# Weights split by columns beside A and B, v by key blocks loaded first, attention spread as 12 places over the first A and 20 over the first B

## The chip, the cores and the metric

The kernel runs on one core of a Trainium2 chip. A core has TensorE (PE: matmuls, with its weight loads listed apart as PEld), VectorE (DVE), ScalarE (ACT), GpSimd (POOL) and SyncE (SP), each with its own queue of instructions, which it works off in order, and 16 DMA engines. SyncE here only issues DMAs. The metric is the device time of one execution in microseconds (us), the median of several runs. The profile is of one such execution.

## What is computed

Three stages, each feeding the next. Attention for 4 batches of 8 heads, 576 positions, head size 64, in two parts that are added: a dense one over positions averaged by fours (144 of them), and a local one in which each query sees the keys less than 4 positions away. Then a gated feed-forward block whose gate is a convolution over 3 positions, then a second one with a causal convolution over 5 positions.

```python
q_d = q.reshape(B, H, Sd, 4, D).mean(axis=3)          # k_d, v_d alike
out_d = sm_attn(q_d, k_d, v_d)                        # 144 x 144 softmax attention
mask = np.abs(pos[:, None] - pos[None, :]) < 4
attn = softmax(where(mask, scale * q @ k.T, -1e9))
x = np.repeat(out_d, 4, axis=2) + attn @ v            # (4, 576, 512) after the heads are joined
h = np.maximum(x @ w_in, 0.0)                         # A: 512 -> 1024
conv_out = sum(conv_w[k] * hp[:, k:k + S] for k in range(3))
y = (h * sigmoid(conv_out)) @ w_out                   # B: 1024 -> 512
gate_pre = sum(conv_w2[k] * yp[:, k:k + S] for k in range(5))
out = (sigmoid(gate_pre) * (y @ w_val)) @ w_out2      # C and D: 512 -> 512 each
```

The weight matrices are 64-bit floats in memory; q, k and v are 32-bit.

## The kernel before

**Precision.** Every large product is made of three: a matrix is split into a high part (rounded to the fast 32-bit matmul type) and a low part (the rest), and high x high, high x low and low x high are summed (`mm3`). A 64-bit weight piece is first turned into a 32-bit float by integer operations (`to_f32`: one ACT and four DVE operations on 128 x 512) and then split by one ACT copy (high) and one DVE subtraction (low). Such a piece with its six operations is called a split below.

**Weights.** The class `Weights` holds a list of jobs, 16 in all: 8 pieces of 128 rows x 512 columns of w_in (tiles win0 and win1 for high and low), then 8 of w_out (wout0, wout1). `load` issues the DMA of the next piece (512 KB) into a staging tile called stage, on SyncE's queue; `split` does the six operations on the oldest staged piece. The staging tiles take turns in the three buffers y1, y2, y3 for the first nine pieces and in y3 and y2 behind that, so a load must wait until the split of the piece that had its buffer is over.

**Attention.** It runs in 16 steps s, one for each pair of heads (4 for each batch), of 8 slots i each (`att_slots`): slot 0 the local scores (sl, 96 small matmuls in a masked PSUM tile), slot 1 the dense scores (sd), slots 2 and 3 the local product with v of the step before (avl, in two halves; it needs the value windows ldw: 32 keys for each block of 24 queries) and the softmax normalisations, slots 4 and 5 the transposes of the next step's k and q (tp) and its pooled values (ldv, vd), slots 6 and 7 the transposes of the probabilities (et, etd) and the dense product (avd). The results are xo, split into xhi and xlo.

**A and B.** For each batch 32 units: A has 16 (8 column blocks f of w_in, two units each; behind the second, ACT and DVE make relu, convolution, gate and the split into hghi and hglo, DVE's part being cv three times and hglo), B has 16 (4 column blocks e of w_out, four units each; the fourth needs hghi and hglo of f = 6 and 7). A matmul of A is called pa, one of B pb. `step_unit` issues one unit, and ahead of it one `split` and one `load` where its rule says so.

**Order.** The main loop at the end runs the steps and slots. With s = 4, i = 5 the first unit is issued, and from there on one unit after each slot: 32 slots for the 32 units of batch 0 beside the attention of batch 1, then 32 slots for those of batch 1, and so on. Ahead of that, the attention of batch 0 runs without units, and `EARLY` names the slots behind which a split and a load are issued. `ordered` makes the instructions that a function issues stand behind the last ones of the named engines. `split` in `step_unit` is called outside of `ordered`, so the tile framework's scheduler places its operations on their engines by its own estimate of when they can run.

**Loads at the start.** Before, SyncE issues k and q of all four head pairs with v in two halves among them, the conv weights, three weight pieces, then `load_vw_first`: 24 loads of 64 KB, the value windows of batch 0 (6 groups g x 4 partition blocks c), then the first loads of batch 1. A DMA queue has 8 semaphores in turn, so a load waits for the eighth before it.

Behind all this (not touched): the units of batches 1 to 3 beside the attention of batches 2 and 3, then C and D.

## Time and profile before

| | us |
|---|---|
| median of 3 runs | 521.6 (517.53 to 523.5) |
| the profiled execution | 523.8 |
| its span, first to last instruction | 521.7 |
| PE busy | 453.0 (87%) |
| PEld busy | 412.7 (79%) |
| DVE busy | 358.2 (69%) |
| ACT busy | 266.0 (51%) |
| POOL busy | 6.1 (1%) |
| the 16 DMA engines, 39.58 MB | 76 GB/s over the span |

Times of rows are counted from the span's start. A row of a timeline gives start, duration, engine, line, operation, output<-inputs, shapes and count; a bracket at its end says how long the engine had stood idle before it and what it waited for. An engine that is busy most of the time need not be what limits a stage; what limits it is read from the chain of waits and from the rows around a wait.

### The profile page before, as it was taken

How to read it: one execution, taken by the hardware profiler on the slowest of the kernel's cores; microseconds unless marked ns; L12 is line 12 of the kernel's file. 1: busy time of each engine (PE TensorE's matmuls, PEld its weight loads, DVE VectorE, ACT ScalarE, POOL GpSimd, SP SyncE). 2: the span in 40 equal slices, each digit the busy share in tenths (PEclk: the TensorE clock that was granted, in tenths of full speed). 3: DMA queues.
4: the chain of work that ended last, by engine and by line, in shares of the span. 5: the costliest groups of instructions: out<-in, count | busy, mean ns of one | idle time of the engine just before them, and what ended most of it. 6: DMA issues, size and time to landing. Idle time of an engine off the chain costs nothing.

```text
span 521.7 us, 13808 instructions
## 1 busy us (share of the span) xinstructions
PE 453.0 (87%) x5961; PEld 412.7 (79%) x5961; DVE 358.2 (69%) x655; ACT 266.0 (51%) x564; POOL 6.1 (1%) x25
## 2 busy tenths in 40 slices
PE   5747565468977999899899999999968999999997
PEld 4546544357976999899899889999958999889885
DVE  3517678789997344897866799503989999964130
ACT  1504535467784443877545678414877365542122
POOL 4000000000000000000000000000000000000000
PEclk9955556598998999999799999999987999999999
DMA  8957124343441214224133121003112000120102
GB/s 204 222 130 164 52 82 114 113 132 111 119 113 29 67 43 93 48 58 98 28 74 79 37 64 32 14 21 122 40 41 81 10 33 2 60 102 20 62 21 102
DMA packets 70963, 39.58 MB, mean 76 GB/s; under 512 B 59050, under 2 KB 65526, under 8 KB 70902
## 3 DMA queue, kind: packets, MB, share of 16 engines
q1 hardware_dynamic: 70902, 38.70, 28.0%
q8 instruction: 47, 0.77, 0.6%
q14 instruction: 14, 0.11, 0.1%
HBM read 33.96 MB, written 4.72 MB: 74 GB/s over the span
## 4 chain that ended last, share of the span: by engine, by line
PE 59%; DVE 21%; DMA 9%; ACT 7%; SPq 2%; issue 1%; ACTq 0%; DVEq 0%
PE pb L141 19%; PE pa L141 12%; PE pc L141 10%; PE pd L141 10%; DVE cv L151 5%; DVE stage L151 4%; PE avl L141 3%; DMA ldv<-in_v_dram 3%; DMA stage<-in_moe_w_in_dram 2%; ACT ed L151 2%; DMA ldq<-in_q_dram 2%; DVE hglo L151 2%; SPq L283 1%; PE tp L141 1%; DMA stage<-in_moe_w_out_dram 1%
## 5 line engine op out<-in xcount | busy, mean ns | idle before, releaser
L141 PE MATMUL pb<-hghi,wout 128*128 128x288 f32 x512 | 105.5, 314 | 4.7 <-ACT hghi L151 4.7
L141 PE MATMUL pa<-xhi,win 128*128 128x288 f32 x512 | 103.0, 308 | 3.6 <-DVE xo L151 3.6
L141 PEld LDWEIGHTS pb<-hghi,wout 128*128 128x128 f32 x512 | 80.6, 197 | 8.6 <-ACT hghi L151 5.6
L141 PEld LDWEIGHTS pa<-xhi,win 128*128 128x128 f32 x512 | 78.1, 192 | 6.9 <-DVE xo L151 3.9
L141 PE MATMUL pb<-hglo,wout 128*128 128x288 f32 x256 | 57.5, 307 | 2.0 <-DVE hglo L151 2.0
L151 DVE SCALAR_TENSOR_TENSOR cv<-h,cwt,cv 128x576 f32<-128x576 f32 x64 | 51.9, 811 | 7.5 <-ACT cv L151 7.1
L141 PE MATMUL pa<-xlo,win 128*128 128x288 f32 x256 | 55.5, 299 | 0.0
L141 PE MATMUL pc<-ys,wval 128*128 128x288 f32 x384 | 51.3, 294 | 0.0
L141 PEld LDWEIGHTS pc<-ys,wval 128*128 128x128 f32 x384 | 51.1, 188 | 0.3
L151 DVE SCALAR_TENSOR_TENSOR g<-y,cwt,g 128x576 f32<-128x576 f32 x64 | 49.5, 814 | 0.0
L141 PEld LDWEIGHTS avl<-et,ldw 32*64 32x64 f32 x1536 | 30.1, 150 | 22.3 <-issue 8.5
L141 PE MATMUL avl<-et,ldw 32*64 32x24 f32 x1536 | 34.2, 227 | 15.5 <-DMA ldw<-in_v_dram 9.2
L141 PEld LDWEIGHTS pb<-hglo,wout 128*128 128x128 f32 x256 | 43.0, 197 | 3.5 <-DVE hglo L151 3.4
L141 PE MATMUL pd<-wout,hghi 128*128 128x512 f32 x144 | 44.7, 394 | 0.0
L141 PEld LDWEIGHTS pa<-xlo,win 128*128 128x128 f32 x256 | 42.0, 193 | 0.0
L151 DVE TENSOR_TENSOR xo<-avl,od 128x288 f32<-128x288 f32 x32 | 14.2, 444 | 32.3 <-PE avl L141 32.3
L151 ACT ACTIVATE ed<-ed,smd 72x144 f32<-72x144 f32 x64 | 21.4, 404 | 23.6 <-DVE smd L151 23.6
L141 PEld LDWEIGHTS pd<-wout,hghi 128*128 128x128 f32 x144 | 26.7, 187 | 6.3
L151 ACT ACTIVATE cv<-cv 128x576 f32<-128x576 f32 x32 | 21.9, 683 | 15.3 <-DVE cv L151 14.9
L151 DVE TENSOR_TENSOR hglo<-cv,hghi 128x576 fp32r<-128x576 f32 x32 | 24.1, 753 | 6.8 <-ACT hghi L151 6.8
L151 ACT ACTIVATE hghi<-cv 128x576 fp32r<-128x576 f32 x32 | 21.8, 680 | 13.0 <-DVE cv L151 12.9
L151 ACT ACTIVATE ed<-sd,mxd 72x144 f32<-72x144 f32 x64 | 23.3, 370 | 10.0 <-DVE mxd L151 9.2
(87 smaller groups left out, 695.2 us busy)
## 6 DMA issues: line engine op xcount, KB each, us to landing
stage<-in_moe_w_out_dram SPq DMA_DIRECT2D x12, 512.0 KB
out_dram<-o SPq DMA_DIRECT2D x18, 256.0 KB
stage<-in_moe_w_in_dram SPq DMA_DIRECT2D x8, 512.0 KB
ldv<-in_v_dram SPq DMA_DIRECT2D x13, 288.0 KB
ldk<-in_k_dram SPq DMA_DIRECT2D x26, 144.0 KB
ldq<-in_q_dram SPq DMA_DIRECT2D x26, 144.0 KB
ldw<-in_v_dram SPq DMA_DIRECT2D x48, 48.0 KB
stage<-in_moe_w_val_dram SPq DMA_DIRECT2D x4, 512.0 KB
```

The lines of the kernel that those rows point to most:

```text
L141: last["pe"] = nc.tensor.matmul(*a, **kw)
L151: last[self.key] = getattr(self.engine, name)(*a, **kw)
L283: nc.sync.dma_start(out=vw[KB * c : KB * c + KB, g], in_=v[0, :, k0 : k0 + KB].rearrange("h k d -> k h d"))
```

## The change

Five edits. The 16 weight pieces are cut by columns: a piece of w_in is now all 512 rows x 128 columns (one f), a piece of w_out 512 of its 1024 rows x 128 columns (half of one e); the bytes of a piece and the operations of a split stay the same, and a load now has 512 runs of 1 KB instead of 128 of 4 KB. The loads of pieces behind the first three are issued by POOL instead of SyncE. At the start, the value windows are loaded behind k and q of the first two head pairs and the first half of v; then come the three weight pieces, then k, q and v of the rest. `EARLY` has 4 entries instead of 8, and the 12 other splits are called at the units in `SPLITS`. The 16 units of batch 0's A are spread over 12 slots and the 16 of its B over 20, instead of 16 and 16; from unit 33 on the slots are the same as before.

```diff
-        def load(self):
+        def load(self, queue=nc.gpsimd):
             if not self.jobs:
                 return
-            dst, src, j, f0 = self.jobs.pop(0)
-            rows = src[j * 128 : j * 128 + 128]
+            dst, src, r0, nr, c0 = self.jobs.pop(0)
+            wide = PW // nr
+            rows = src[r0 * 128 : (r0 + nr) * 128]
...
-                nc.sync.dma_start(out=t, in_=rows.bitcast(I32)[:, 2 * f0 : 2 * (f0 + PW)])
-            self.staged.append((t, w, src.dtype == F32, dst, j, f0))
+                queue.dma_start(
+                    out=t.rearrange("p (r n) -> p r n", r=nr),
+                    in_=rows.bitcast(I32).rearrange("(r p) n -> p r n", p=128)[
+                        :, :, 2 * c0 : 2 * (c0 + wide)
+                    ],
+                )
...
-            hi, lo = dst[0][:, j, f0 : f0 + PW], dst[1][:, j, f0 : f0 + PW]
-            self.parts(w, hi, lo)
+            hi, lo = (d[:, r0 : r0 + nr, c0 : c0 + PW // nr] for d in dst)
+            self.parts(w.rearrange("p (r n) -> p r n", r=nr), hi, lo)
...
-    for hp in range(HP):
+    for hp in range(2):
         load(k, "ldk", 0, hp)
         load(q, "ldq", 0, hp)
-        if hp % 2 == 0:
-            load_v_first(hp // 2)
+        if hp == 0:
+            load_v_first(0)
+    load_vw_first()
...
-    W = Weights([(win, w_in), (wout, w_out)], stage)
-
+    W = Weights(
+        [(win, w_in, 0, KM, f * 128) for f in range(KF)]
+        + [(wout, w_out, r, KF // 2, e * 128) for e in range(KM) for r in (0, KF // 2)],
+        stage,
+    )
+
+    for _ in range(3):
+        W.load(nc.sync)
+    for hp in range(2, HP):
+        load(k, "ldk", 0, hp)
+        load(q, "ldq", 0, hp)
+        if hp == 2:
+            load_v_first(1)
...
-    for _ in range(3):
-        W.load()
-    load_vw_first()
...
-        if W.staged and (b > 0 or m % 2 == 0) and "ep" not in E:
+        if b == 0 and m in SPLITS:
             W.split()
             W.load()
...
-    EARLY = [(1, 5), (2, 1), (2, 3), (2, 5), (3, 1), (3, 3), (3, 5), (3, 7)]
+    EARLY = [(1, 5), (2, 1), (2, 5), (3, 3)]
+    SPLITS = (1, 3, 5, 7, 10, 12, 14, 16, 18, 20, 22, 24)
...
             if (s, i) > (HP, 4):
-                step_unit()
+                slot += 1
+                due = slot if slot > 32 else slot * 16 // 12 if slot < 12 else 16 + (slot - 12) * 16 // 20
+                while pos < due:
+                    step_unit()
```

Three places show how the instructions move. The first is SyncE's queue at the start, in the program's order; k, q and v are ldk, ldq and ldv, the value windows ldw, the conv weights cw. Before, from the first load of v on:

```order
L270 DMA ldv<-in_v_dram 72x8x256
L252 DMA ldk<-in_k_dram 96x2x384
L252 DMA ldq<-in_q_dram 96x2x384
L252 DMA ldk<-in_k_dram 96x2x384
L252 DMA ldq<-in_q_dram 96x2x384
L270 DMA ldv<-in_v_dram 72x8x256
L252 DMA ldk<-in_k_dram 96x2x384
L252 DMA ldq<-in_q_dram 96x2x384
L794 DMA cw<-in_moe_conv_w_dram 24x256
L794 DMA cw<-in_moe_conv_w_dram 20x256
L215 DMA stage<-in_moe_w_in_dram 128x1024 x3
L283 DMA ldw<-in_v_dram 32x8x64 x24
```

Now, from the same load of v on:

```order
L274 DMA ldv<-in_v_dram 72x8x256
L256 DMA ldk<-in_k_dram 96x2x384
L256 DMA ldq<-in_q_dram 96x2x384
L287 DMA ldw<-in_v_dram 32x8x64 x24
L214 DMA stage<-in_moe_w_in_dram 128x4x256 x3
L256 DMA ldk<-in_k_dram 96x2x384
L256 DMA ldq<-in_q_dram 96x2x384
L274 DMA ldv<-in_v_dram 72x8x256
L256 DMA ldk<-in_k_dram 96x2x384
L256 DMA ldq<-in_q_dram 96x2x384
L810 DMA cw<-in_moe_conv_w_dram 24x256
L810 DMA cw<-in_moe_conv_w_dram 20x256
```

The 24 loads of the value windows and the three weight pieces moved ahead of k and q of the third and fourth head pair and of the second half of v.

The second place is ACT in the third step of batch 0's attention, from the copy of the transposed k (kT) to the exponentials of the dense scores (ed from sd). A number behind stage tells pieces apart: before, stage_154, stage_545 and stage_653 are the third, fourth and fifth piece, in buffers y3, y1 and y2. Before:

```order
L151 ACTIVATE stage_154<-stage_154 128x512
L151 ACTIVATE kT_742<-tp_729 128x576
L151 ACTIVATE qT_762<-tp_749 128x576
L151 ACTIVATE stage_545<-stage_545 128x512
L151 ACTIVATE etd_785<-etd_786 72x576
L151 ACTIVATE od_801<-avd_796 128x144
L151 ACTIVATE win0_75<-stage_154 128x512
L151 ACTIVATE win0_75<-stage_545 128x512
L151 ACTIVATE el_805<-el_805 128x384
L151 ACTIVATE ed_862,smd_861<-sd_863,mxd_860 72x144 x4
L151 ACTIVATE stage_653<-stage_653 128x512
```

Now stage_167 is the third piece (y3), and stage_653, stage_772 and stage_1222 are the fifth (y2), sixth (y3) and eighth (y2); all three are loaded by POOL:

```order
L151 ACTIVATE kT_733<-tp_720 128x576
L151 ACTIVATE stage_653<-stage_653 128x512
L151 ACTIVATE qT_753<-tp_740 128x576
L151 ACTIVATE stage_167<-stage_167 128x512
L151 ACTIVATE etd_776<-etd_777 72x576
L151 ACTIVATE od_792<-avd_787 128x144
L151 ACTIVATE win0_75<-stage_653 128x4x128
L151 ACTIVATE win0_75<-stage_167 128x4x128
L151 ACTIVATE el_796<-el_796 128x384
L151 ACTIVATE stage_1222<-stage_1222 128x512
L151 ACTIVATE ed_853,smd_852<-sd_854,mxd_851 72x144 x4
L151 ACTIVATE stage_772<-stage_772 128x512
```

The fifth piece stands ahead of the third and directly behind kT, and the eighth, which takes the buffer that the fifth leaves, stands ahead of the exponentials; before, the fifth stood behind them.

The third place is DVE at the end of batch 0's A, around the subtraction that makes hglo of the last f (the hglo that follows the last cv). Before:

```order
L151 TENSOR_REDUCE kd_1907<-kT_1905 128x144
L151 SCALAR_TENSOR_TENSOR stage_1600<-stage_1600 128x512
L151 TENSOR_TENSOR hglo_1969<-cv_1839,hghi_1968 128x576
L151 TENSOR_REDUCE qd_1953<-qT_1951 128x144
L151 SCALAR_TENSOR_TENSOR cv_1939<-h1_79,cwt_74,cv_1939 128x576
L151 TENSOR_TENSOR wout1_1224<-stage_1600,wout0_1223 128x512
L151 SCALAR_TENSOR_TENSOR cv_1939<-h1_79,cwt_74,cv_1939 128x576
L151 TENSOR_TENSOR vd_2273<-ldv_1961 72x256
L151 SCALAR_TENSOR_TENSOR cv_1939<-cv_1939,h1_79 128x576
L151 TENSOR_TENSOR ldv_2278<-ldv_2278 72x4x128
L151 TENSOR_TENSOR hglo_1969<-cv_1939,hghi_1968 128x576
L151 TENSOR_REDUCE mxl_2033<-sl_2036 128x12
```

Now:

```order
L151 TENSOR_TENSOR hglo_1859<-cv_1696,hghi_1858 128x576
L151 SCALAR_TENSOR_TENSOR cv_1796<-cv_1796,h1_79 128x576
L151 TENSOR_TENSOR xlo_1846<-xo_1815,xhi_77 128x576
L151 TENSOR_REDUCE kd_1932<-kT_1930 128x144
L151 TENSOR_TENSOR hglo_1859<-cv_1796,hghi_1858 128x576
L151 TENSOR_SCALAR stage_1957<-stage_1957 128x512 x2
L151 TENSOR_REDUCE qd_1982<-qT_1980 128x144
L151 SCALAR_TENSOR_TENSOR stage_1957<-stage_1957 128x512 x2
L151 TENSOR_TENSOR vd_2286<-ldv_1990 72x256
L151 TENSOR_TENSOR wout1_1188<-stage_1957,wout0_1187 128x4x128
L151 TENSOR_TENSOR ldv_2291<-ldv_2291 72x4x128
L151 TENSOR_REDUCE mxl_2047<-sl_2050 128x12
```

The last split, qd, vd and the addition on ldv moved from in front of that hglo to behind it.

## Rows read from the trace of the kernel before

**Rows 1.** Chain of work that ended last: start us, us, what.
```profile
14.62 11.93 DMA stage<-in_moe_w_in_dram
...
35.04 1.99 DMA ldw<-in_v_dram
```

**Rows 2.** Timeline of TensorE, 22 to 52 us; columns as told above.
```profile
22.35 1.14 PE L141 MATMUL sd<-kd,qd 64*72 64x144 f32 x8
...
38.60 2.19 PE L141 MATMUL tp<-ident,ldk 96*64 96x96 f32 x24
...
51.01 2.39 PE L141 MATMUL avl<-et,ldw 32*64 32x24 f32 x96
```

**Rows 3.** Timeline of SyncE's queue (issues, not transfers), 0 to 36 us.
```profile
0.74 0.39 SPq L252 DMA_DIRECT2D ldk<-in_k_dram  x1
...
19.77 16.21 SPq L283 DMA_DIRECT2D ldw<-in_v_dram  x24
```

**Rows 4.** DMA issues: tensor, queue, count, KB each.
```profile
stage<-in_moe_w_in_dram SPq DMA_DIRECT2D x8, 512.0 KB
...
ldw<-in_v_dram SPq DMA_DIRECT2D x24, 64.0 KB
ldk<-in_k_dram SPq DMA_DIRECT2D x4, 288.0 KB
...
ldv<-in_v_dram SPq DMA_DIRECT2D x2, 576.0 KB
```

**Rows 5.** Timeline of DVE and ACT, 58 to 73 us.
```profile
58.07 0.69 DVE L151 TENSOR_TENSOR win<-stage,win 128x512 fp32r<-128x512 f32 x1
...
61.32 0.66 ACT L151 ACTIVATE stage<-stage 128x512 f32<-128x512 f32 x1
...
61.88 0.63 ACT L151 ACTIVATE kT<-tp 128x576 f32<-128x576 f32 x1
...
68.20 0.69 DVE L151 TENSOR_TENSOR win<-stage,win 128x512 fp32r<-128x512 f32 x1
...
72.32 0.38 ACT L151 ACTIVATE ed<-sd,mxd 72x144 f32<-72x144 f32 x1 [0.42 <-DVE mxd L151]
```

**Rows 6.** Chain of work that ended last, 90 to 184 us.
```profile
90.16 3.57 DMA stage<-in_moe_w_out_dram
...
96.01 3.68 DMA stage<-in_moe_w_out_dram
...
183.78 1.17 PE sl L141 x63
```

**Rows 7.** Timeline of ACT and TensorE, 99 to 102 us.
```profile
99.77 0.66 ACT L151 ACTIVATE stage<-stage 128x512 f32<-128x512 f32 x1 [3.35 <-DMA stage<-in_moe_w_out_dram]
...
101.31 0.85 PE L141 MATMUL pa<-xhi,win 128*128 128x288 f32 x2 [3.61 <-DVE xo L151]
```

**Rows 8.** Chain of work that ended last: a load of ldv (288 KB).
```profile
108.54 4.28 DMA ldv<-in_v_dram
```

**Rows 9.** Windows: stretch, length, busy us (and instructions) of each engine, granted clock, DMA share, GB/s.
```profile
105.50:166.50 61.00, 49.97 (x798) 45.41 (x798) 56.60 (x108) 40.70 (x84) 0.11 (x1) 0.94 0.37 101
166.50:197.00 30.50, 30.46 (x495) 28.40 (x496) 14.50 (x33) 13.15 (x37) 0.00 (x0) 1.00 0.22 52
```

**Rows 10.** Timeline of DVE and TensorE, 165 to 167 us.
```profile
165.13 0.69 DVE L151 TENSOR_TENSOR ldv<-ldv 72x512 f32<-72x512 f32 x1 [2.27 <-DMA ldv<-in_v_dram]
...
166.54 0.54 PE L141 MATMUL pb<-hglo,wout 128*128 128x288 f32 x2 [0.43 <-DVE hglo L151]
```

**Rows 11.** Groups by line and shape: busy us, mean ns of one.
```profile
L151 DVE SCALAR_TENSOR_TENSOR stage<-stage 128x512 int32<-128x512 int32 x32 | 21.7, 680 | 0.2
...
L151 DVE TENSOR_SCALAR stage<-stage 128x512 f32<-128x512 f32 x16 | 6.7, 418 | 6.9 <-ACT stage L151 6.9
```

**Rows 12.** Timeline of TensorE, 155 to 160 us.
```profile
155.06 0.70 PE L141 MATMUL etd<-ident,ed 72*72 72x72 f32 x8 [1.22 <-ACT kT L151]
...
159.66 1.13 PE L141 MATMUL avd<-etd,vd 72*64 72x144 f32 x8 [2.28 <-ACT etd L151]
```

More of the change, by code (lines that the diff above doesn't have):

```diff
@@ L194, in __init__ @@
         def __init__(self, jobs, stage):
-            self.jobs = [
-                (dst, src, j, f0)
-                for dst, src in jobs
-                for f0 in range(0, src.shape[1], PW)
-                for j in range(src.shape[0] // 128)
-            ]
+            self.jobs = jobs
             self.stage = stage
@@ L212, in load @@
             if src.dtype == F32:
-                nc.sync.dma_start(out=w, in_=rows[:, f0 : f0 + PW])
-            else:
-                nc.sync.dma_start(out=t, in_=rows.bitcast(I32)[:, 2 * f0 : 2 * (f0 + PW)])
-            self.staged.append((t, w, src.dtype == F32, dst, j, f0))
+                queue.dma_start(
+                    out=w.rearrange("p (r n) -> p r n", r=nr),
+                    in_=rows.rearrange("(r p) n -> p r n", p=128)[:, :, c0 : c0 + wide],
+                )
+            else:
+                queue.dma_start(
+                    out=t.rearrange("p (r n) -> p r n", r=nr),
[3 more added lines that the diff above has]
+                )
+            self.staged.append((t, w, src.dtype == F32, dst, r0, nr, c0))
         def split(self):
@@ L220, in split @@
                 return
-            t, w, plain, dst, j, f0 = self.staged.pop(0)
+            t, w, plain, dst, r0, nr, c0 = self.staged.pop(0)
             if not plain:
                 to_f32(vec, act, w, t.rearrange("p (n t) -> p n t", t=2))
-            hi, lo = dst[0][:, j, f0 : f0 + PW], dst[1][:, j, f0 : f0 + PW]
-            self.parts(w, hi, lo)
+            hi, lo = (d[:, r0 : r0 + nr, c0 : c0 + PW // nr] for d in dst)
+            self.parts(w.rearrange("p (r n) -> p r n", r=nr), hi, lo)
         @staticmethod
@@ L783, in stage @@
         return t[:, : 2 * PW], t[:, 2 * PW :].bitcast(F32)
-    W = Weights([(win, w_in), (wout, w_out)], stage)
+    W = Weights(
+        [(win, w_in, 0, KM, f * 128) for f in range(KF)]
+        + [(wout, w_out, r, KF // 2, e * 128) for e in range(KM) for r in (0, KF // 2)],
+        stage,
+    )
+    for _ in range(3):
[5 more added lines that the diff above has]
+            load_v_first(1)
     nw = 3 * KF + 5 * KM
@@ L841 @@
     ALL = ("pe", "vec", "act")
-    EARLY = [(1, 5), (2, 1), (2, 3), (2, 5), (3, 1), (3, 3), (3, 5), (3, 7)]
+    EARLY = [(1, 5), (2, 1), (2, 5), (3, 3)]
+    SPLITS = (1, 3, 5, 7, 10, 12, 14, 16, 18, 20, 22, 24)
     ordered(lambda: prep_k(0), ALL)
     ordered(lambda: prep_q(0), ALL)
+    slot = 0
     for s in range(NSTEP + 1):
```

## Prediction

> **What bounds the kernel now.** I read the page's chain first, then the timeline of the first 110 us by engine, then the windows around the first A and B, because the change ends where the 32 units of batch 0 end. The kernel has three stretches there. Up to 38.6 us it waits for DMA: the chain runs through the last weight load, which lands at 26.55, and then through ldw, which lands at 37.03 [rows 1]. TensorE finished the score matmuls sd at 23.49 and could not begin the next transposes until 38.60, because the 48 avl matmuls ahead of them needed ldw, the value windows [rows 2]. With ldw at hand a whole avl pair takes 2.39 us [rows 2]. SyncE issued the 24 ldw loads from 19.77 on, behind all of k, q, v and three weight pieces [rows 3].
>
> From 38.6 to 101.3 (the first pa [rows 7]) the attention of batch 0 runs as one chain that alternates DVE, ACT and TensorE, with the weight splits put in between on DVE and ACT. A late weight piece stops this chain: twice the chain goes through a stage load of 3.57 and 3.68 us from issue to use, and in front of the second ACT stands idle for 3.35 us [rows 6, 7].
>
> From 105.5 to 166.5 DVE bounds: 56.6 of 61.0 us busy, at 49.97 for TensorE [rows 9]. It ends with the hglo of the last f, for which TensorE waits at 166.54 [rows 10]. From there to 197.0 TensorE bounds, 30.46 of 30.50 us busy while DVE has 14.5 [rows 9]. Behind 197 the unit order is the old one, so I carry the sum on unchanged.
>
> **(a) Loads at the start.** ldw goes from the end of the start queue to behind k, q of the first two head pairs and half of v; the three weight pieces and then k, q of head pair 2 follow. Before, 8 x 288 (four ldk, and four ldq of the same shape) + 2 x 576 + 3 x 512 + 24 x 64 = 6528 KB [rows 4] landed between the first issue at 0.74 [rows 3] and 37.03: 180 KB/us. After, k of head pair 2 is the last of 4 x 288 + 576 + 24 x 64 + 3 x 512 + 288 = 5088 KB, which at that rate is 28.3 us, at 29.0. Slow end: 4992 KB without ldw had landed by 26.55, so 193 KB/us for large pieces; 1728 KB in 9.0, ldw at the 16.2 us that its issues took [rows 3] with nothing beside it, 1824 KB in 9.5: 35.4. Fast end: no DMA wait, 23.49 + 2.39 = 25.9. I take 31.0, nearer to the mean rate, since the first ldw loads are issued while the big ones still move. So the wait for ldw goes, and the wait that stands next is that of the transposes for k of head pair 2: 38.6 becomes 31.0, **-7.6 us** (-12.7 to -3.2). The conv weights move behind all of k and q, 6528 KB in, 37 at the mean rate; ACT wants them 7.4 us behind that transpose in the trace of before, at 38.4. I cost that at nothing; the cover is 1.4 us.
>
> **(b) The splits of batch 0's attention.** The smaller table of early splits looks as if it halved this work. The order says no: the splits in the A/B loop are bound to no place, and the scheduler pulls them forward, so that ahead of the first cv the same 8 of w_in and 2 to 3 of w_out stand on DVE as before. Only 0.4 of a split more lies before the first A. A split is 2 x 0.42 + 2 x 0.68 [rows 11] + 0.69 for the subtraction [rows 5] = 2.9 us of DVE: **+1.1 us**.
>
> What changes is who is late. The loads now leave from POOL, each when its buffer is free, and the queue of SyncE no longer stands behind them. The order is another: stage_653 and stage_1222 sit in one buffer, and ACT's first operation on each stands near the split that frees it. For stage_653 the split ends at 58.76, and ACT comes to the piece at 61.9, behind the kT copy that started at 61.88 and now goes first at 61.32 [rows 5]: 3.1 us. For stage_1222 the freeing subtraction answers to the one that ends at 68.89; the exponentials of ed follow at 72.32, one operation of 0.6 fewer between, so 2.8 us, and the piece's own 0.66 now stands in front of them [rows 5]. With T for the time from free buffer to landed piece, the two stalls are T - 3.1 and T + 0.66 - 2.8. The next four loads have 4.5 to 6 us by the same count, so they add about 4 x (T - 5) above 5 us.
>
> No row shows a load from POOL. Low end: the 3.6 us of the same bytes from SyncE [rows 6]. High end: ldv, also in pieces of 1 KB, took 4.28 us for 288 KB [rows 8]; by bytes 7.6 for 512 KB. I take 5.0, between them and nearer to the row of equal size. Stalls: 1.9 + 2.9 = 4.8 (2.0 at 3.6, 20.4 at 7.6). Of the waits of before, I count 2.5 of ACT's 3.35 us as gone. (b) is 1.1 + 4.8 - 2.5 = **+3.4 us** (0 to +19).
>
> The Trainium skill, "DMA: Bandwidth & Descriptors", section "Anatomy of one DMA — SWDGE (gpsimd) path", fits a load from POOL by about 2.0 us plus bytes over 436 GB/s; that is an estimate of 3.2 us for 512 KB, by which the two stalls would be 1.2, (b) -0.2 and the time 511.2. No row here shows such a load, and the 3.57 us of the same bytes from SyncE is already longer than that fit.
>
> **(c) A over 12 places, B over 20.** In DVE's order, four things that stood before the last hglo of A now stand behind it: one split (2.9), qd, vd and the ldv addition (some 1.6 together), and with that addition its 2.27 us wait for DMA [rows 10]. A rest of a split (0.6) went to (b). Operations overlap a little, so DVE's 61.0 us become about 54.5: **-6.5**. They land where DVE has 16 us free [rows 9]. TensorE, however, must still run 12 units of B after that hglo, as before, with 3 slots of attention more, since the fourth unit of B stood in slot 20 and now stands in slot 17: etd 0.70 [rows 12], avd taken as the same, sl 1.17 [rows 6], together 2.6. And etd and avd now stand without a unit between, so avd waits for ACT's copy between them: before, with a unit between, it waited 2.28 us at worst [rows 12] and at other places not at all; I take 1.3. That is **+3.9**. (c) is **-2.6 us** (-5 to +2).
>
> **Sum.** -7.6 + 3.4 - 2.6 = -6.8 us. Against the profiled execution, 523.8 us with a span of 521.7 and 2.1 around it, that is 517.0. It is 2.2 above the median of the three runs, so I state the prediction on the median: 521.6 - 6.8 = **514.8 us**. A change under 1%, 5.2 us, is what a measurement of this kernel can hardly tell from none.
>
> **Rivals.**
> The forecast, a gain of 2 to 11 us: chance 0.50.
>
> The loads from POOL are late (ends slower): the place is ACT's row for stage_653 and stage_1222, then stage_1268, 937, 1384 and 1656. The gain of 6.8 holds stalls of 4.8; they reach 11.6, and the sum zero, at T = 6.1 (3.0 + 4.0 + 4 x 1.1 = 11.4). At T = 6.6 they are 3.5 + 4.5 + 6.4 = 14.4, and the time is 521.6 - 7.6 + 1.1 + 14.4 - 2.5 - 2.6 = 524.4. For it: 4.28 us for a little more than half the bytes in pieces of this size [rows 8], and two loads often in flight together. Against: 3.6 us for the same bytes alone [rows 6]. Chance 0.18.
> A rule for it stands in the Trainium skill, "SBUF — State Buffer", section "SBUF: two separate sides": descriptors of a load from POOL are written by GpSimd over a port that some DVE operations hold, so such a load waits for DVE; by that rule T lies above SyncE's 3.6. In the trace of before POOL does nothing beside DVE at these places, so no run here shows it.
>
> The start moves by the full mean rate and the loads are quick: k of head pair 2 at 29.0 (-9.6), T = 3.6 (b 0.6), (c) as above: -11.6, 510.0. For it: 180 KB/us is measured over the same mix. Chance 0.20.
>
> The change doesn't do what it says: ldw is as slow in front as behind and everything behind it moves back, k at 35.4 (-3.2): -2.4, 519.2. For it: ldw's issues, not its bytes, set 16.2 us [rows 3]. Chance 0.12.
>
> **How the numbers follow.** 514.8 is that of the likeliest. Faster by over 1% are the rival at 510 and two thirds of the forecast's chance: 0.53. Within 1%: the rest of the forecast, the 519.2 case and a third of the late loads, 0.35. Slower: 0.12, the rest of the late loads. The range leaves out the deep end of both: 508 to 523. The likeliest's own range is 511 to 519.
>
> **What would show it.** (a) The avl of head pair 0 starts near 23.5 without a DMA wait, and the transposes of head pair 2 start near 31 behind DMA ldk or ldq; at 26 or at 35 the term is wrong. (b) The idle time of ACT in front of stage, put down to DMA stage<-in_moe_w_in_dram, is 4 to 6 us up to the first pa, which stands near 97; over 10 us is the first rival. (c) From the first pa to the last pb of batch 0 takes some 93 us instead of 95.7; from the last hglo on TensorE is busy throughout. If DVE's operations become longer beside POOL's loads, or the time behind the last pb of batch 0 changes, the prediction is wrong in a way that I haven't priced.

## The result and the profile after

The changed kernel takes 514.3 us (median of 12 runs, 512.7 to 518.0), the one before 521.4 in the same comparison (one of its 12 runs, of 1365 us, is not in the ratio): ratio 0.9873, 95% interval 0.9849 to 0.9897. That is 6.6 us off (5.4 to 7.9), more than the 1% told in the prediction. The profiled execution took 514.15 us with a span of 512.4, against 523.8 and 521.7.

Five moments tell most of the story. All times are from profiled executions, one of each kernel; the ratio is that of the timed runs to those of the kernel before. The labels E1 to E12 are the experiments below.

| | tp for k of head pair 2 | first pa | last hglo of A begins | first pa of batch 1 | first pa of batch 2 | span | ratio (95%) |
|---|---|---|---|---|---|---|---|
| before | 38.60 | 101.31 | 165.74 | 196.80 | 280.57 | 521.7 | 1 |
| after | 32.67 | 95.77 | 152.10 | 190.03 | 270.97 | 512.4 | 0.9873 (0.9849 to 0.9897) |
| E1 | 31.70 | 92.80 | 157.50 | 188.52 | 270.05 | 511.5 | 0.9887 (0.9853 to 0.9922) |
| E2 | 27.19 | 93.96 | 151.95 | 189.32 | 270.18 | 512.1 | 0.9887 (0.9852 to 0.9922) |
| E3 | 36.23 | 98.83 | 160.02 | 197.39 | 278.18 | 519.7 | 1.0050 (1.0027 to 1.0072) |
| E4 | 32.69 | 96.90 | 153.59 | 192.05 | 275.61 | 516.9 | 0.9882 (0.9846 to 0.9919) |
| E5 | 31.58 | 93.57 | 158.37 | 190.61 | 271.50 | 513.7 | 0.9917 (0.9879 to 0.9955) |
| E6 | 33.64 | 93.39 | 152.19 | 193.44 | 273.98 | 515.7 | 0.9878 (0.9842 to 0.9914) |
| E7 | 29.04 | 95.13 | 152.21 | 190.45 | 271.38 | 513.0 | 0.9825 (0.9790 to 0.9860) |
| E8 | 26.68 | 92.91 | 157.73 | 189.16 | 272.06 | 513.2 | 0.9843 (0.9804 to 0.9882) |
| E9 | 33.40 | 103.03 | 158.57 | 200.12 | 280.73 | 522.5 | 1.0012 (0.9986 to 1.0039) |
| E10 | 27.33 | 98.72 | 156.20 | 196.85 | 277.66 | 519.2 | 1.0013 (0.9985 to 1.0040) |
| E11 | 28.62 | 91.06 | 153.16 | 185.78 | 267.87 | 509.5 | 0.9792 (0.9763 to 0.9820) |
| E12 | 27.67 | 89.24 | 150.69 | 188.22 | 268.58 | 510.3 | 0.9842 (0.9798 to 0.9886) |

**The start.** Timeline of SyncE, then of TensorE and ACT, of the changed kernel:

```profile
3.12 18.85 SPq L287 DMA_DIRECT2D ldw<-in_v_dram  x24
22.01 1.56 SPq L214 DMA_DIRECT2D stage<-in_moe_w_in_dram  x3
23.61 0.50 SPq L256 DMA_DIRECT2D ldk<-in_k_dram  x1
```

```profile
23.10 2.39 PE L141 MATMUL avl<-et,ldw 32*64 32x24 f32 x96
32.67 2.19 PE L141 MATMUL tp<-ident,ldk 96*64 96x96 f32 x24 [7.19 <-DMA ldk<-in_k_dram]
...
57.01 0.66 ACT L151 ACTIVATE stage<-stage 128x512 f32<-128x512 f32 x1 [1.50 <-DMA stage<-in_moe_w_in_dram]
...
68.28 0.66 ACT L151 ACTIVATE stage<-stage 128x512 f32<-128x512 f32 x1 [2.16 <-DMA stage<-in_moe_w_in_dram]
71.04 0.67 ACT L151 ACTIVATE stage<-stage 128x512 f32<-128x512 f32 x1 [0.66 <-DMA stage<-in_moe_w_in_dram]
...
95.77 0.85 PE L141 MATMUL pa<-xhi,win 128*128 128x288 f32 x2 [2.42 <-DVE xo L151]
...
153.92 0.67 ACT L151 ACTIVATE stage<-stage 128x512 f32<-128x512 f32 x1 [2.27 <-DMA stage<-in_moe_w_out_dram]
...
156.25 1.23 PE L141 MATMUL avd<-etd,vd 72*64 72x144 f32 x8 [1.41 <-ACT etd L151]
```

The wait for ldw [rows 2] is gone: the 96 avl start at 23.10 with no bracket. What stands next is k of head pair 2, issued only at 23.61, behind the 24 issues of ldw. It starts at 32.67, 5.9 us earlier than before. Three loads of weight pieces then stop ACT for 4.3 us in sum up to the first pa, and one more, the last piece, behind A. Windows of the kernel before, then of the changed one, columns as in [rows 9] (busy time of TensorE, its weight loads, DVE, ACT and POOL, then clock, DMA share and GB/s): from the second step to the first pa, and for the changed kernel the stretches around the last hglo:

```profile
38.00:101.30 63.30, 36.44 (x802) 29.90 (x798) 48.97 (x112) 29.06 (x74) 0.00 (x0) 0.53 0.43 111
```

```profile
32.70:95.80 63.10, 36.84 (x776) 30.25 (x776) 46.98 (x104) 26.66 (x68) 5.39 (x7) 0.50 0.50 128
95.80:152.90 57.10, 48.81 (x697) 44.84 (x697) 54.59 (x103) 41.13 (x87) 4.72 (x7) 0.94 0.34 98
...
150.00:153.00 3.00, 1.44 (x7) 0.97 (x7) 2.85 (x5) 1.64 (x3) 0.10 (x1) 1.00 0.66 210
153.00:156.00 3.00, 1.84 (x12) 1.52 (x12) 1.34 (x3) 2.08 (x4) 0.00 (x0) 0.56 1.10 170
156.00:159.00 3.00, 2.75 (x14) 2.37 (x15) 2.57 (x5) 1.00 (x3) 0.00 (x0) 0.50 0.01 5
```

In A, DVE still bounds (54.59 of 57.10 us, against 56.6 of 61.0 in [rows 9]). Behind it TensorE is not busy throughout: 1.44 of 3.0 us while it waits for the last hglo, 1.84 of 3.0 while ACT waits for the last piece, and from about 153 to 160 its granted clock is at 0.5, the lower level of 1.2 GHz.

### The profile page after: what moved, and what is told of

Read it like the earlier page. It is cut to its first block, busy times and chain, and to the rows that moved or that the text cites. A ratio compares the mean times of both kernels' runs of the same rounds, so it can differ in the third digit from the quotient of the medians.

```text
span 512.4 us, 13822 instructions
## 1 busy us (share of the span) xinstructions
PE 446.8 (87%) x5961; PEld 407.8 (80%) x5961; DVE 357.6 (70%) x655; ACT 266.2 (52%) x564; POOL 16.1 (3%) x38
## 4 chain that ended last, share of the span: by engine, by line
PE 51%; DVE 22%; DMA 13%; ACT 7%; SPq 3%; issue 3%; POOL 0%; ACTq 0%; POOLq 0%
PE pb L141 16%; PE pc L141 10%; PE pd L141 10%; PE pa L141 8%; DVE cv L151 7%; DMA ldv<-in_v_dram 5%; DVE stage L151 3%; DMA ldk<-in_k_dram 3%; DMA ldq<-in_q_dram 2%; DVE hglo L151 2%; ACT ed L151 2%; DMA stage<-in_moe_w_in_dram 2%; PE avl L141 2%; SPq L287 2%; PE tp L141 1%
## 5 line engine op out<-in xcount | busy, mean ns | idle before, releaser
L141 PE MATMUL pa<-xhi,win 128*128 128x288 f32 x512 | 101.1, 306 | 2.4 <-DVE xo L151 2.4
L141 PEld LDWEIGHTS avl<-et,ldw 32*64 32x64 f32 x1536 | 28.3, 154 | 15.0 <-DVE xo L151 4.9
L141 PE MATMUL avl<-et,ldw 32*64 32x24 f32 x1536 | 31.2, 230 | 9.0 <-DVE xo L151 4.2
L141 PE MATMUL pd<-wout,hglo 128*128 128x512 f32 x72 | 28.3, 395 | 0.0
L151 DVE SCALAR_TENSOR_TENSOR gvf<-g,pc 128x576 f32<-128x576 f32 x16 | 12.0, 752 | 22.5 <-PE pc L141 22.5
L151 ACT ACTIVATE cv<-cv 128x576 f32<-128x576 f32 x32 | 21.8, 680 | 11.3 <-DVE cv L151 11.2
```

The source lines that it names most:

```text
L141: last["pe"] = nc.tensor.matmul(*a, **kw)
L151: last[self.key] = getattr(self.engine, name)(*a, **kw)
```

## Experiments

**E1: only the order of the start loads.** The kernel before, with the instructions of TensorE, DVE and ACT in their old order; row pieces, all from SyncE.

```diff
-    for hp in range(HP):
+    for hp in range(2):
         load(k, "ldk", 0, hp)
         load(q, "ldq", 0, hp)
...
+    load_vw_first()
...
+    for _ in range(3):
+        W.load(nc.sync)
+    for hp in range(2, HP):
+        load(k, "ldk", 0, hp)
...
-    for _ in range(3):
-        W.load()
-    load_vw_first()
```

> The kernel before with the new order of the start loads in SyncE's queue and nothing else: row pieces, the old table of splits, 16 places over A and 16 over B; the order on TensorE, DVE and ACT is that of before. Theory: term (a) is a wait for loads and carries through. The transposes for k of head pair 2 start at 32.7 us as in the changed kernel (38.6 before), the first pa near 95.5 (101.3), and the time is 521.4 - 5.9 = 515.5 us. Rival 1: the weight pieces, still issued by SyncE behind the start loads, come later than the attention now wants them and give back half or more: first pa behind 98, time over 518. Rival 2: (a) was not the gain of the changed kernel at all; then 521.

Measured: 514.8 us, ratio 0.9887, -5.9 us (-7.7 to -4.1). Timeline of TensorE in E1, and the window between the two rows:

```profile
31.70 2.19 PE L141 MATMUL tp<-ident,ldk 96*64 96x96 f32 x24 [6.31 <-DMA ldk<-in_k_dram]
...
92.80 0.85 PE L141 MATMUL pa<-xhi,win 128*128 128x288 f32 x2 [3.54 <-DVE xo L151]
```

```profile
31.70:92.80 61.10, 36.88 (x776) 30.24 (x776) 46.22 (x103) 27.27 (x69) 0.00 (x0) 1.00 0.53 132
```

The theory holds, and more: the order of the loads alone gives the changed kernel's time within the intervals. Row pieces or column pieces, SyncE or POOL, the tables and the places together are worth 0.7 us, with an interval of over 2 us to each side; none of the runs has the column pieces alone. From tp to the first pa it takes 61.1 us here and 62.7 before, with the same order and nearly the same waits of ACT for pieces (4.1 and 4.3 us). DVE has some 2 us less to do in it (46.22 against 48.97 in a stretch begun 0.6 us earlier): the last operations of the attention's first step, which before stood behind the wait for ldw, now run while tp waits for k. TensorE's clock differs too, at its upper level through this stretch here and mostly at its lower one before. How much of the 1.6 us comes from either, these two executions don't tell.

**E2: k and q of head pair 2 ahead of ldw** on the changed kernel, second half of v right behind ldw; the order on TensorE, DVE and ACT is that of the changed kernel.

```diff
-    for hp in range(2):
+    for hp in range(3):
         load(k, "ldk", 0, hp)
...
     load_vw_first()
+    load_v_first(1)
```

> The changed kernel with k and q of head pair 2 issued ahead of ldw, and the second half of v right behind ldw, ahead of the weight pieces; the order on TensorE, DVE and ACT stays. Theory: what stood next after ldw, the 7.2 us wait of the transposes for ldk, comes from the 24 issues of ldw and the three pieces ahead of it; with k ahead of them the transposes follow the avl of head pair 0 at once, near 27 instead of 32.7. The first pa stands near 91 and the time is 514.3 - 5 = 509 us. Rival 1: the wait moves on to ldw or to the weight pieces and cw, so that the second step still begins its splits at 37: 513 to 514. Rival 2: the bytes limit, k of head pair 2 at 27 makes k of head pair 3 or the pieces later by the same time: 513 to 515.

Measured: 514.6 us, ratio 0.9887. Timeline of TensorE and ACT in E2:

```profile
27.19 2.19 PE L141 MATMUL tp<-ident,ldk 96*64 96x96 f32 x24
...
39.53 0.31 ACT L151 ACTIVATE cw<-cw 44x128 f32<-44x128 f32 x1 [3.58 <-DMA cw<-in_moe_conv_w_dram]
55.55 0.66 ACT L151 ACTIVATE stage<-stage 128x512 f32<-128x512 f32 x1 [1.81 <-DMA stage<-in_moe_w_in_dram]
...
93.96 0.85 PE L141 MATMUL pa<-xhi,win 128*128 128x288 f32 x2 [2.45 <-DVE xo L151]
```

The 7.2 us wait is gone and tp stands 5.5 us earlier, but the first pa only 1.8 and that of batch 1 only 0.7. Rival 1 comes nearest: the conv weights, loaded last, now stop ACT for 3.58 us, and the pieces for 5.3 in sum against 4.3.

**E3: only the places, 12 and 20,** on the kernel before.

```diff
             if (s, i) > (HP, 4):
-                step_unit()
+                slot += 1
+                due = slot if slot > 32 else slot * 16 // 12 if slot < 12 else 16 + (slot - 12) * 16 // 20
+                while pos < due:
+                    step_unit()
```

> The kernel before with 12 places over A and 20 over B, the old start order, row pieces, SyncE for all loads, the old table of splits. Theory: term (c) is worth what the two profiles show between the first pa of batch 0 and that of batch 1, 95.7 to 94.5, -1.2 us, of which the half-speed stretch of TensorE at 153 to 160 takes some 3: so 520 us, and 517 if that stretch is not there. Rival: the whole of (c) comes from the later splits, the places alone move nothing or cost: 521.4 or more.

Measured: 524.4 us, ratio 1.0050 (1.0027 to 1.0072): 2.6 us slower. The rival is right for the places alone. From the first pa to the last hglo it is 61.2 us instead of 64.4, so 3.2 won; behind that, up to the first pa of batch 1, 37.4 instead of 31.1, so 6.3 lost.

**E4: pieces from SyncE** on the changed kernel.

```diff
-        def load(self, queue=nc.gpsimd):
+        def load(self, queue=nc.sync):
```

> The changed kernel with all weight pieces issued by SyncE instead of POOL; the order that the scheduler makes on DVE and ACT changes with it. Theory: POOL's loads cost little, 4.1 to 4.3 us from issue to landing against 3.6 for SyncE's, so this moves under 2 us either way by that: 512.5 to 515.5; what speaks against it is that on SyncE a piece stands behind ldk and ldv loads that wait for their buffers. Rival 1: POOL's way is what lets the pieces come in time: idle time of ACT in front of stage over 10 us up to the first pa, time 518 or more. Rival 2: POOL's loads hold up DVE, and without them the time falls by over 2 us.

Measured: 514.6 us, ratio 0.9882; nothing to tell it from the changed kernel (0.9873). Neither rival holds. Which queue issues the pieces makes no difference that these intervals, some 2 us to each side, could show; the scheduler's order moves a little with it.

**E5: 16 places and 16** on the changed kernel.

```diff
-                due = slot if slot > 32 else slot * 16 // 12 if slot < 12 else 16 + (slot - 12) * 16 // 20
+                due = slot
```

> The changed kernel with one unit for each slot of attention, 16 places over A and 16 over B as before, and all else changed. Theory: (c) is worth what the two profiles show between the first pa of batch 0 and that of batch 1 (95.5 before, 94.3 after), so without it the first pa stays at 95.8, that distance goes to 95.5 or a little more, and the time is 515.5. Rival 1: the places cost here as they did alone, 2.8 us, and the kernel without them takes 511.5. Rival 2: with the splits of w_out cut by columns the places are worth the whole 8 us by which the stretch from the first pa to the last hglo of A became shorter: 520.

Measured: 516.8 us, ratio 0.9917, 2.3 us above the changed kernel by the ratios, though the intervals overlap. From first pa to first pa it takes 97.0 us (94.3 with 12 and 20). That is nearest to the theory. Here the places seem to help, by an amount that the runs don't separate from none; in E3 they hurt clearly.

**E6: the old tables** on the changed kernel: 8 early splits, then one at every second unit.

```diff
-        if b == 0 and m in SPLITS:
+        if W.staged and (b > 0 or m % 2 == 0) and "ep" not in E:
...
-    EARLY = [(1, 5), (2, 1), (2, 5), (3, 3)]
+    EARLY = [(1, 5), (2, 1), (2, 3), (2, 5), (3, 1), (3, 3), (3, 5), (3, 7)]
```

> The changed kernel with the old table of 8 early splits and the old rule, a split at every second unit, and all else changed. Theory: the scheduler puts the splits where it wants anyway, so the tables move under 1.5 us: first pa 95 to 97, time 513 to 516. Rival: the smaller table is what spares DVE splits ahead of the first pa; with 8 early splits the first pa is 4 x 2.9 us of DVE work later or part of it, and the time 518 or more.

Measured: 515.6 us, ratio 0.9878: the total is as the theory says, the way there is not. ACT waits for no piece at all up to the first pa, which comes at 93.39 (95.77 in the changed kernel). 8 splits are finished ahead of it instead of 7, and yet DVE has less work on pieces there, 24.4 us against 25.7, since in the changed kernel three more are nearly finished by then. Behind the first pa ACT waits 9.7 us in six places in A and B, and from first pa to first pa it takes 100.1 us. The order on ACT tells why the waits moved; these are its first conversions in the changed kernel, numbered in the order in which the pieces are loaded by the program:

```
stage_163 stage_165 stage_653 stage_167 stage_1222 stage_772 stage_545
```

The program loads 163, 165, 167, 545, 653, 772, 937, 1222. With the new table the scheduler splits the fifth piece ahead of the third, and the fourth, which POOL issues first, as the seventh. So ACT waits for a fresh piece (653, 1222) while landed ones lie in their buffers. With the old table the first nine come in order.

**E7: E2 with cw behind ldw as well;** the loop that loads it moves up.

```diff
     load_vw_first()
+    for src, o, m in ((conv3, 0, 3 * KF), (conv5, 3 * KF, 5 * KM)):
...
     load_v_first(1)
```

> The changed kernel with k and q of head pair 2 ahead of ldw, as in the run before, and now cw and the second half of v right behind ldw as well. Theory: in the run with k of head pair 2 ahead, ACT waited 3.58 us for cw and DVE 3.02 behind it, which took back most of the 5.5 us won at the transposes; with cw ahead the first pa comes near 90.5 (93.96 there, 95.77 in the changed kernel). From there to the first pa of batch 1 it takes 94.5 to 95.5 as in both, and the time is 511. Rival: TensorE and DVE limit A and B by other loads with a time of their own (ldv, the pieces of w_out), so the first pa of batch 1 stays near 189.5 and the time at 514.

Measured: 512.9 us, ratio 0.9825 (0.9790 to 0.9860), 2.5 us below the changed kernel by the ratios, with intervals that overlap a little. The profiled execution does not show where: it is one of the longer ones, with the first pa at 95.13. Timeline of TensorE and ACT in E7:

```profile
27.51 1.60 PE L141 MATMUL avl<-et,ldw 32*64 32x24 f32 x52 [2.32 <-DMA ldw<-in_v_dram]
...
55.71 0.66 ACT L151 ACTIVATE stage<-stage 128x512 f32<-128x512 f32 x1 [3.31 <-DMA stage<-in_moe_w_in_dram]
...
66.86 0.66 ACT L151 ACTIVATE stage<-stage 128x512 f32<-128x512 f32 x1 [2.04 <-DMA stage<-in_moe_w_in_dram]
```

The wait for cw is gone, and the pieces take its place: 6.7 us in sum up to the first pa. The time lies between the theory (511) and the rival (514).

**E8: E1 with the loads ordered as in E7.**

```diff
-    for hp in range(2):
+    for hp in range(3):
...
     load_vw_first()
+    for src, o, m in ((conv3, 0, 3 * KF), (conv5, 3 * KF, 5 * KM)):
...
+    load_v_first(1)
```

> The kernel before with only the order of the start loads changed, and that as in the run above: k and q of three head pairs, ldw, cw, second half of v, the three weight pieces, the rest. The order on TensorE, DVE and ACT is that of before. Theory: the wait of 6.3 us for ldk that the run with only the changed order of the start still showed goes, first pa near 88 (92.8 there), distance to the first pa of batch 1 95.7 as there, time 510. Rival 1: the weight pieces from SyncE come too late for the earlier attention and ACT waits for them over 4 us more: 513 to 515. Rival 2: the same limit behind the first pa as in the run above: 514.

Measured: 514.1 us, ratio 0.9843, 2.3 us below E1 by the ratios, not separated. Tp stands at 26.68 (E1: 31.70), the first pa where it was (92.91 and 92.80). ACT waits 10.9 us for pieces, 4.48 of them at 56.44: rival 1.

**E9 and E10: a fourth buffer for the pieces,** on the changed kernel and on E7; the fourth piece is loaded at the end of the start queue.

```diff
-        t = keep.tile([128, 3 * PW], I32, tag=f"y{1 + n % 3 if n < 9 else 2 + n % 2}", name="stage")
+        tag = ("y1", "y2", "y3", "g")[n % 4] if n < 8 else ("y2", "y3", "g")[(n - 8) % 3]
+        t = (mp if tag == "g" else keep).tile([128, 3 * PW], I32, tag=tag, name="stage")
...
+    W.load(nc.sync)
     load_v(1, 0)
```

> The changed kernel with a fourth buffer for weight pieces (the space that batch 0's C uses much later), a fourth piece loaded at the end of the start queue, so every later piece is loaded one split earlier. The scheduler orders the splits somewhat differently with it. Theory: what was left behind the start are waits for pieces whose load goes out when a split frees its buffer: ACT 1.50 + 2.16 + 0.66 us up to the first pa, 1.20 in A and 2.27 behind the last hglo of A. With a buffer more these go: first pa near 92.5, ACT's waits for pieces under 1 us, time 510. Rival: the waits are the price of POOL's queue, whose loads stand in order behind one that waits for its buffer; then they stay above 3 us and the time is 513.5 or more.

> The four buffers together with k and q of head pair 2, cw and the second half of v ahead of the weight pieces. Theory: in the run with these loads ahead, ACT's waits for pieces had grown to 3.31 + 2.04 + 1.39 us up to the first pa and 2.39 us behind A, which took back what the start had won; with the fourth buffer the first pa comes near 88 and the time is 506 to 508. Rival: DVE's own work sets the time to the first pa, 47 us busy between the second step and it; then first pa is 92 or later and the time 511 or more.

Measured: 521.9 and 522.2 us, ratios 1.0012 and 1.0013: the whole gain is lost. Timeline of ACT and TensorE in E9:

```profile
49.58 0.66 ACT L151 ACTIVATE stage<-stage 128x512 f32<-128x512 f32 x1 [3.70 <-DMA stage<-in_moe_w_in_dram]
...
77.03 0.66 ACT L151 ACTIVATE stage<-stage 128x512 f32<-128x512 f32 x1 [3.02 <-DMA stage<-in_moe_w_in_dram]
...
103.03 0.85 PE L141 MATMUL pa<-xhi,win 128*128 128x288 f32 x2 [4.74 <-DVE xo L151]
```

The theory fell. With a free buffer the scheduler puts even more fresh pieces first: the second conversion on ACT is the piece that POOL issues at 44.35, while older ones lie in their buffers. ACT waits 8.9 us for pieces up to the first pa (11.3 in E10; 4.3 in the changed kernel). DVE's work on pieces there grows by 0.8 us only, from 25.7 to 26.5; 8 splits are finished, not the 9 of which the expectation of E12 speaks.

**E11: the same four buffers and start order on the kernel before,** where the pieces are split in order (the edits of E8 and E9 together).

> The kernel before (row pieces, all loads by SyncE, old tables, 16 places and 16) with the order of the start loads of the run above and the four buffers. Theory: as above the pieces were what the earlier start waited for (2.08 + 4.48 + 0.88 + 3.43 us of ACT up to the first pa), first pa near 88, time 508. Rival: SyncE's queue, where pieces stand behind ldk, ldq and ldv that wait for their buffers, keeps them late: ACT's waits above 5 us and time 513 or more.

Measured: 511.5 us, ratio 0.9792 (0.9763 to 0.9820), 10.8 us less than before and below the changed kernel's interval; it has the lowest median of all, though E7's interval overlaps with its own. Timeline of ACT and TensorE in E11:

```profile
83.70 0.66 ACT L151 ACTIVATE stage<-stage 128x512 f32<-128x512 f32 x1 [0.83 <-DMA stage<-in_moe_w_out_dram]
...
91.06 0.85 PE L141 MATMUL pa<-xhi,win 128*128 128x288 f32 x2 [3.48 <-DVE xo L151]
```

ACT's waits up to the first pa fall from 10.9 us (E8) to 0.83. The theory of E9 holds once the pieces come in order, though the first pa stands at 91, not 88: from tp to it 62.4 us are left with next to no wait for a piece.

**E12: E10 with the old tables** (the edit of E6), so that column pieces, POOL and the places 12 and 20 meet pieces in order.

> The run with four buffers and k, q of head pair 2, cw and the second half of v ahead, on top of the changed kernel, now with the old table of 8 early splits and a split at every second unit. With the old table the scheduler splits the pieces in the order in which they are loaded; with the new one it splits the fifth ahead of the third and the fourth as the seventh, so a fresh piece is waited for while landed ones lie in their buffers. Theory: that order, not the fourth buffer, made the two four-buffer runs on the changed kernel slow (9 splits ahead of the first pa, 8.9 and 11.3 us of ACT's waits for pieces). In order, ACT waits under 1 us up to the first pa, which stands near 90; the places 12 and 20 give their 2.3 us, and the time is 509 to 511, against 511.5 of the four buffers on the kernel before. Rival: POOL's queue or the places cost with in-order pieces too; ACT's waits stay above 3 us, or the time is 513 or more.

Measured: 512.2 us, ratio 0.9842 (0.9798 to 0.9886), 9 us below E10 by the ratios: with the old tables, which put the pieces in order, the loss is gone, so it was not the fourth buffer by itself that cost E9 and E10 their time. ACT waits 1.53 us up to the first pa, at 89.24, the earliest of all. The rest of the theory fell: the places give nothing that shows (the intervals of E11 and E12 overlap). Window of E12 behind the last hglo:

```profile
150.00:160.00 10.00, 8.29 (x134) 7.12 (x135) 2.06 (x4) 2.25 (x4) 0.00 (x0) 0.66 0.30 74
```

From first pa to first pa it takes 99.0 us, 4.3 more than E11, and TensorE is again at its lower clock right behind the last hglo.

## Why the prediction was right, point by point

The time (514.8 against 514.3) and the sign hold, and so does the mechanism of (a), which by E1 is worth the whole gain within the intervals. The terms of the sum are off by up to 3 us and cancel; that the total came within 1 us is luck. By the two profiles the sum is -5.9 for (a), +0.4 for (b), -1.2 for (c) and -2.8 for something that it didn't price, together -9.5, against 9.3 us between the spans.

**(a), -7.6 forecast, -5.9 measured.** The wait for ldw goes and k of head pair 2 is next, at 32.67 instead of 31.0. (The avl ahead of these transposes are 96, not the 48 that the prediction names; nothing hangs on it.) The term that was mis-sized is the rate. Windows of the first 24 us, before and after:

```profile
0.00:24.00 24.00, 16.53 (x324) 13.99 (x324) 11.09 (x24) 8.23 (x21) 5.62 (x21) 1.00 0.91 220
```

```profile
0.00:24.00 24.00, 16.58 (x361) 13.80 (x361) 11.37 (x24) 8.40 (x21) 5.62 (x21) 0.78 0.69 150
```

With ldw ahead 150 GB/s are moved in that time, where the big loads moved 220. The 24 issues take 18.85 us, more than the 16.21 of [rows 3], and k is issued at 23.61. The prediction's slow end had reckoned with such issues and gave 35.4, but set them behind 9 us of large loads; they began at 3.12, beside those, and k then needed 9.1 us together with the pieces ahead of it. The conv weights at nothing held, with a cover so thin that E2 ran into it. E1, with this order alone, is faster by 5.9 us.

**(b), +3.4 forecast, +0.4 measured.** The two stalls named were 1.9 and 2.9 us and came as 1.50 and 2.16, at the pieces and in the order forecast; with 0.66 at a third, ACT's idle time was 4.3 (4 to 6 forecast). T, the time from a free buffer to a landed piece, was taken as 5.0. The page's list of DMA issues of the changed kernel, with the median us from issue to landing at the end, and the chain's steps of these loads:

```profile
stage<-in_moe_w_out_dram POOLq DMA_DIRECT2D x8, 512.0 KB, 4.1
...
stage<-in_moe_w_in_dram POOLq DMA_DIRECT2D x5, 512.0 KB, 4.3
```

```profile
52.63 4.29 DMA stage<-in_moe_w_in_dram
64.80 6.16 DMA stage<-in_moe_w_in_dram
...
149.35 4.49 DMA stage<-in_moe_w_out_dram
```

Alone a load takes 4.1 to 4.5 us; 6.2 is the second of two issued together. That is longer than SyncE's 3.6 [rows 6]. The Trainium skill, "DMA: Bandwidth & Descriptors", section "Anatomy of one DMA — SWDGE (gpsimd) path", gives an estimate of 3.2 us for such a load. These rows exceed it by about 1 us.

The step that failed is what goes away. Before, ACT's waits for pieces up to the first pa were 0.98 us, in the row below, and the 3.35 of [rows 7], and all of it went, not 2.5.

```profile
93.81 0.66 ACT L151 ACTIVATE stage<-stage 128x512 f32<-128x512 f32 x1 [0.98 <-DMA stage<-in_moe_w_out_dram]
```

The added work of DVE came as forecast, +1.0 against +1.1. Windows with the instructions on the staging tiles alone (DVE, then ACT, then POOL where it has any), before and after:

```profile
38.00:101.30 63.30, 24.66 (x46) 12.06 (x19) 0.53 0.43 111
```

```profile
32.70:95.80 63.10, 25.68 (x47) 11.33 (x18) 5.39 (x7) 0.50 0.50 128
```

Of DVE's 47 operations now, 35 are 7 whole splits and 12 belong to three that lack only the subtraction; of the 46 before, 40 are 8 whole splits. That the same splits stand ahead of the first cv was right. By these terms (b) would be 1.0 + 4.3 - 4.3 = +1.0. Something that the sum didn't have works the other way: DVE's whole work in the stretch falls, from 48.97 to 46.98 us (windows above), because the end of the attention's first step, some 3 us of DVE, now runs while tp waits for k, as in E1. Its last operation, on xlo, stood behind the start of tp before (38.60) and stands ahead of it now (32.67):

```profile
42.26 0.76 DVE L151 TENSOR_TENSOR xlo<-xo,xhi 128x576 fp32r<-128x576 f32 x1 [2.03 <-ACT xhi L151]
```

```profile
29.39 0.76 DVE L151 TENSOR_TENSOR xlo<-xo,xhi 128x576 fp32r<-128x576 f32 x1 [2.03 <-ACT xhi L151]
```

That can account for the 0.6 us between 1.0 and the measured 0.4, but the traces don't show how much of it reaches the first pa.

The prediction also took the tables to be without effect. In the time they are (E6), but not in the order: the new one makes fresh pieces come before landed ones. That is what the two stalls were, and the prediction had the signs of it (two pieces in one buffer, each converted near the split that frees it) without the cause.

**(c), -2.6 forecast, -1.2 measured.** Both halves were too small. The stretch up to the last hglo shrank by 8.1 us (64.4 to 56.3; forecast 6.5). What comes behind it grew by 6.9 (31.1 to 37.9; forecast 3.9). "TensorE is busy throughout from the last hglo on" was wrong. Windows from the last hglo to the first pa of batch 1, before, after, and in E4:

```profile
165.70:196.80 31.10, 30.67 (x498) 28.37 (x497) 15.30 (x35) 12.95 (x37) 0.00 (x0) 1.00 0.21 50
```

```profile
152.10:190.00 37.90, 35.30 (x609) 32.30 (x609) 19.79 (x43) 15.34 (x42) 0.00 (x0) 0.91 0.31 70
```

```profile
153.60:192.00 38.40, 33.90 (x618) 31.25 (x617) 19.72 (x43) 15.53 (x42) 0.00 (x0) 1.00 0.34 79
```

Of the growth, 4.6 us are busy time of TensorE and 2.2 are idle time. The larger part of the idle time is the wait of avd (1.3 forecast, 1.41 measured). Of the busy time the three slots were to take 2.6; of the other 2.0 the lower clock seems to have most. From about 153 to 160, right after 3 us of which it was busy 1.44, TensorE runs at the lower level; in E4, which stays at the upper one here, it is busy 1.4 us less, with a few matmuls more. E4's stretch is no shorter for it: ACT waits 3.58 us for a piece there, and TensorE stands idle for 4.5. The table shows that this half belongs to the places, whatever else is in the kernel, and that the first half needs the late splits as well:

| places, tables | kernels | first pa to last hglo | last hglo to first pa of batch 1 | sum |
|---|---|---|---|---|
| 16 and 16, old | before, E1, E8, E11 | 62.1 to 64.8 | 31.0 to 32.6 | 94.7 to 96.3 |
| 16 and 16, new | E5 | 64.8 | 32.2 | 97.0 |
| 12 and 20, old | E3, E6, E12 | 58.8 to 61.5 | 37.4 to 41.3 | 98.6 to 100.1 |
| 12 and 20, new | after, E2, E4, E7 | 56.3 to 58.0 | 37.4 to 38.5 | 94.3 to 95.4 |
| 12 and 20, new, four buffers | E9, E10 | 55.5 to 57.5 | 40.6 to 41.6 | 97.1 to 98.1 |

**Behind batch 0.** The prediction carried the sum on unchanged from 197 us. From the first pa of batch 1 to that of batch 2 it is 83.8 us before and 80.9 after. Windows from the first pb of batch 1 to the first pa of batch 2, before, after, and in E1:

```profile
237.10:280.60 43.50, 42.09 (x656) 39.18 (x654) 32.55 (x60) 23.11 (x55) 0.00 (x0) 0.92 0.27 62
```

```profile
230.20:271.00 40.80, 38.97 (x657) 36.23 (x654) 32.16 (x60) 22.98 (x55) 0.00 (x0) 1.00 0.27 65
```

```profile
228.40:270.00 41.60, 40.40 (x654) 37.51 (x652) 32.27 (x60) 23.21 (x55) 0.00 (x0) 0.96 0.27 63
```

The work of DVE and ACT is the same; the granted clock is not. The mean of 0.92 over 43.5 us before is 6.8 us at the lower level, 0.96 in E1 is 3.4, and after there is none. E4, a near copy of the changed kernel, is at the lower level for as long there:

```profile
232.00:275.60 43.60, 41.93 (x657) 39.04 (x656) 32.42 (x60) 23.09 (x55) 0.00 (x0) 0.92 0.26 62
```

In all 14 profiles the stretch between these two pa goes with the clock: 80.4 to 80.9 us in the nine without a drop, 81.5 and 82.1 with 3.4 us at the lower level (E1, E11), 82.9 to 83.8 with 6.8 us (E8, E4, before). The drop has one place, 54 to 56 us behind the first pa of batch 1. TensorE has just stood idle ahead of avl there, for 1.20 to 1.41 us in the five kernels with a drop and 1.00 to 1.25 in the nine without. The four kernels with the old pieces, tables and places all have it; of the ten others only E4 does. So the 2.8 us are the clock's; whether the change took the drop away or only this execution missed it, one profile of each kernel does not settle. Part of the 9.3 us between the spans is the execution all the same: the medians differ by 7.1, and the profiled execution before took 523.8 us against a median of 521.4.

**The rivals.** POOL's loads were not late as a rule: 4.1 to 4.5 us against the 6.1 at which the gain would have been gone, and E4, with SyncE in POOL's place, takes the same time within the intervals. The rule of the Trainium skill behind it, "SBUF — State Buffer", section "SBUF: two separate sides", would also let a POOL operation hold up DVE. By groups and shapes, DVE's operations on the pieces in the changed kernel are

```profile
L151 DVE SCALAR_TENSOR_TENSOR stage<-stage 128x512 int32<-128x512 int32 x32 | 21.6, 681 | 0.2
L151 DVE TENSOR_SCALAR stage<-stage 128x512 f32<-128x512 f32 x16 | 6.7, 420 | 9.1 <-ACT stage L151 9.1
```

against 680 and 418 ns in [rows 11]: nothing of it is seen on DVE. Nor do the runs of 1 KB explain that POOL's loads take 0.5 to 0.9 us more than SyncE's. In E4 SyncE issues the same runs, and these are the three quickest of the five such loads in its chain (the others took 5.26 and 6.31):

```profile
63.41 3.63 DMA stage<-in_moe_w_in_dram
72.76 3.55 DMA stage<-in_moe_w_out_dram
87.66 3.63 DMA stage<-in_moe_w_in_dram
```

That is what runs of 4 KB took before (3.57 and 3.68). So the rest goes with POOL: its issue alone lasts 0.75 us where SyncE's lasts 0.4. Whether such a lock has a part in it, no run here shows. The rival at 510 (k at 29.0) and that at 519 (35.4) bracket what came, 32.67.

## What to carry to other kernels

A wait at the head of a queue is worth what stands next: behind ldw stood k, behind k the conv weights, behind those the weight pieces, and taking a wait out gave back little of it as long as the next one stood there: nothing in time for 7.2 us at k in E2, 2.5 us in E7 with the conv weights moved as well, 2.3 us for 6.3 in E8. With all of them out of the way (E11) the kernel is 10.8 us faster than before. When a scheduler places the work that uses prefetched buffers, look in its order whether the buffers are used in the order in which they are filled; a further buffer made the kernel with the wrong order 7 us slower, and with the right order it is in the kernel with the lowest median. And a table of places and a table of splits that are changed together have to be tried apart and together: the places cost 2.6 us with the old tables, and with the new ones they went with a gain of 2.3 us, which the runs don't separate from none.

## What the runs showed of the hardware

TensorE's lower clock costs time where TensorE bounds. In batch 1, where it is busy 39 of 41 us, 6.8 us at the lower level went with a stretch 2.0 to 2.8 us longer (before, E4, E8) and 3.4 us with one 0.6 to 1.2 us longer (E1, E11) than that of the changed kernel. The mean clock of a whole execution says little of its time. Over 63 executions of the kernel before, the mean granted clock lay between 0.88 and 0.98, and the median time was 521.3 us in the ten above 0.96 and 521.8 in the 48 below 0.93.

The 24 ldw loads of 64 KB hold SyncE for 16.2 us before and 17.4 to 19.9 in the kernels with the new start order, and less is moved in that time than by the large loads (150 GB/s against 220 in the first 24 us). Whether their number, their short rows or the wait of each for the eighth load before it makes them dear, no run here tells apart.
